# Storing a whole tile at once near the end: two stores fewer and other completion counters for the last two

## The chip, the cores and the metric

The kernel runs on one core of a Trainium2 chip. The metric is the time of one execution on the device in microseconds (us); three runs of the kernel before took 392.55, 392.9 and 393.38 us. Inside the core several engines work side by side, each with its own instruction stream: TensorE (PE, matrix products; PEld is its weight load), VectorE (DVE), ScalarE (ACT), GpSimd (POOL) and SyncE (SP). SP computes nothing here; it issues transfers and waits. ACT can issue transfers too. The transfers themselves are carried out by 16 DMA engines. Engines and transfers are ordered by semaphores, which are counters that one side raises and the other waits for.

## What is computed

The reference is attention followed by a gated two-layer network:

```python
scores = (1.0 / np.sqrt(q.shape[-1])) * np.matmul(q, k.transpose(0, 1, 3, 2))
scores = scores - np.max(scores, axis=-1, keepdims=True)
attn = np.exp(scores)
attn = attn / (np.sum(attn, axis=-1, keepdims=True) + 1e-09)
attn_out = np.matmul(attn, v)                     # 8 batches, 12 heads, 448 tokens, 64
x = attn_out.transpose(0, 2, 1, 3).reshape(8 * 448, 12 * 64)
h = x @ w_in                                      # 3584 x 2048
g = h * (1.0 / (1.0 + np.exp(-h)))
out = g @ w_out                                   # 3584 x 768, float32
```

## The kernel before

A small planner inside the kernel (class `Order`) walks through time with estimated costs, decides which engine does which operation next, and emits the instructions in that order. The order that comes out is fixed when the program is built. The work runs from attention, batch by batch, through the first product (`w_in`) and the gate to the second product (`w_out`), which is the only part that the change and the prediction touch.

The second product is organised in 14 quads, numbered `qd` = 0 to 13 (`LAST` is 13). A quad covers two tiles of 128 token rows (`i` = 0 and 1) and both halves of the 768 output columns (`j` = 0 and 1, 384 columns each), so it yields four output tiles of 128 rows by 384 columns in float32. Instead of eight blocks of products a quad uses seven, in the manner of a fast 2 by 2 matrix product; `product` (its matmuls all carry line 492) accumulates each into a PSUM bank. An output tile then comes into SBUF as an `ost` tile in up to two steps: `take_copy` (ACT, line 768) copies a bank, `take_sum` (DVE, line 774) adds a second bank in place. Three of the four tiles are finished by a sum; the tile (1, 0), the last one of a quad, is finished by the copy of product 4. The step that finishes a tile calls `store` at once.

`store` (lines 745 to 763) cuts the 128 rows into 4 pieces of 32 rows, because the tokens of batches 0 to 6 are held in another order than in `out`: a group of 32 rows goes to every 14th row. In batch 7, the last one, the tokens are in natural order, so neighbouring pieces can go out together, 64 rows at a time. Tiles are counted within pairs of batches (896 rows, 7 tiles), so that the tiles of the last pair are: tiles 0 to 2 in batch 6, tile 3 half in batch 6 and half in batch 7, and tiles 4 to 6 wholly in batch 7. Tile 3 and tile 4 belong to quad 12, tiles 5 and 6 to quad 13. The stores of quads 12 and 13 alternate between SP and ACT as issuing engine (the expression for `eng` in line 760); all earlier ones are issued by SP.

Each of these stores carries one of eight completion counters, here called counter 0 to 7; the framework gives them out in turn, in program order. A store raises its counter by 16 in all when its data has landed, and before it is issued, the issuing engine waits until the previous store on the same counter has landed. After the last instruction of the kernel the framework adds an end sequence (all of it has line 1554): SP waits, in a fixed order and two counters at a time, for every semaphore of the program, first for two counters of GpSimd's transfers, then for counters 0, 1, 2 and so on to 7 of the stores, each paired with another semaphore. Then it waits once more for GpSimd, and then all engines meet at a barrier, the semaphores are cleared, and they meet again. In the kernel before, the last two stores of the program (the two halves of the last tile) carry counter 0 (the one from ACT) and counter 1 (the one from SP).

Of the kernel before, what the change touches and what calls it, by code (L numbers as in the profile page):

```python
# [169 lines left out]
def kernel(  # L170
# [44 lines left out]
    LAST = NT * B // 4 - 1  # L215
# [514 lines left out]
    def take_plain(t, j):  # L730
        nc.scalar.copy(out=ost(t // 2, t % 2, j), in_=pr_t[("o", t, j)][:, 0:OH])
        store(t // 2, t % 2, j)
# [14 lines left out]
    def store(qd, i, j):  # L747
        u, t = divmod(2 * qd + i, NT)
        w, turn = 0, 0
        while w < 4:  # L750
            r, col = divmod(128 * t + 32 * w, S)
            b = 2 * u + r
            dst = out[b * S : (b + 1) * S, OH * j : OH * (j + 1)]
            if b == B - 1:
                n = 2
                dst = dst[col : col + 32 * n]
            else:
                n = 1
                dst = dst.rearrange("(i g) m -> g i m", g=TPP)[col // 32]
            eng = nc.scalar if turn % 2 and 4 * qd + 8 >= NT * B else nc.sync  # L760
            eng.dma_start(out=dst, in_=ost_t[(qd, i, j)][32 * w : 32 * (w + n), :])
            w, turn = w + n, turn + 1
# [4 lines left out]
    def take_copy(qd, m):  # L767
        nc.scalar.copy(out=ost(qd, *OUT[m]), in_=bank(qd, BANK[m]))  # L768
        if m == 4:
            store(qd, *OUT[m])  # L770

    def take_sum(qd, m):
        t = ost_t[(qd, *SUM[m])]
        nc.vector.tensor_tensor(out=t, in0=bank(qd, BANK[m]), in1=t, op=ALU.add)  # L774
        store(qd, *SUM[m])
# [697 lines left out]
    while True:  # L1473
# [44 lines left out]
        if warm["on"] and od.free["PE"] <= od.now and wait > 0.06 and od.now > 0.9:  # L1518
            each = mm(128) if od.now > COLD else 0.107
            n = max(1, int((wait - 0.06) / each), int(wait / each + 0.9) * (od.now < COLD))  # L1520
            if warm.pop("first", None):
                n = FIRST
# [36 lines left out]
```

## Time and profile before

| | |
|---|---|
| three runs | 392.55, 392.9, 393.38 us; median 392.9 |
| time of the profiled execution | 392.49 us |
| span of the profiled execution, first to last instruction | 390.7 us |
| TensorE busy (matmul) | 384.3 us, 98% of the span |
| VectorE, ScalarE, GpSimd busy | 274.6, 253.7, 89.1 us |
| stores of `out` by SP | 194 of 48 KB, 8 of 96 KB |
| stores of `out` by ACT | 2 of 48 KB, 6 of 96 KB |

The span leaves out 1.79 us of the profiled execution's own time (392.49 - 390.7), which lie before its first and after its last recorded instruction. The views give times from the start of the span. A row of the timeline shows start, duration, engine, line, operation, destination and source, count, and in brackets how long the engine had been idle and what ended it; an engine's name with a `q` stands for its sequencer, the part that issues transfers and waits for semaphores. The duration of a transfer's row there is that of its issue, not of its data. "To landing" is the time from the start of the issue until the counter has its full value.

### The profile page before, as it was taken

The page shows a single profiled execution, that of the slowest core. Times are in us where ns is not written, and L with a number is a line of the kernel's source. Part 1 is how long each engine was busy: PE and PEld are TensorE (multiplying, and loading weights), DVE is VectorE, ACT ScalarE, POOL GpSimd, SP SyncE. Part 2 cuts the span into 40 slices and gives each one's busy share as a digit, 9 for nine tenths or more (in the row PEclk, how much of TensorE's full clock was granted, in tenths as well). Part 3 has the DMA queues.
Part 4 walks back from the last instruction along what each step waited for, and adds up shares of the span by engine and source line. Part 5 has one row for each costly group of instructions (what it writes and reads, how often), then busy time and mean ns, then how long its engine had stood idle before and what let it go on. Part 6 is the DMA issues. An engine that isn't in the chain of part 4 may idle for free.

```text
span 390.7 us, 10672 instructions
## 1 busy us (share of the span) xinstructions
PE 384.3 (98%) x4369; PEld 206.3 (53%) x4369; DVE 274.6 (70%) x570; ACT 253.7 (65%) x399; POOL 89.1 (23%) x173
## 2 busy tenths in 40 slices
PE   8999999999999999999999999999999999999995
PEld 7667774444454444545445444544445655556663
DVE  2466676999996877987588758666869984447441
ACT  4988885697766779666774676466783238882220
POOL 7632365415006243400643014000000000000000
PEclk9999999999999999999999999999999999999999
DMA  7999999929039582814956139002100131001333
GB/s 114 202 210 210 159 161 190 187 42 139 1 62 151 121 105 40 119 47 89 145 82 88 40 73 168 7 0 59 27 0 3 42 93 29 0 3 41 92 95 98
DMA packets 35361, 34.52 MB, mean 88 GB/s; under 512 B 11376, under 2 KB 33776, under 8 KB 35312
## 3 DMA queue, kind: packets, MB, share of 16 engines
q0 software_dynamic: 24784, 22.82, 39.5%
q1 hardware_dynamic: 9952, 10.33, 9.8%
q8 instruction: 34, 0.56, 0.6%
q10 hardware_dynamic: 576, 0.69, 0.6%
q14 instruction: 15, 0.12, 0.1%
HBM read 45.61 MB, written 11.01 MB: 145 GB/s over the span
## 4 chain that ended last, share of the span: by engine, by line
PE 97%; DMA 1%; ACT 1%; issue 0%; POOL 0%; DVE 0%; POOLq 0%
PE p L492 31%; PE h L492 29%; PE s L346 13%; PE a L409 11%; PE f L492 8%; PE o L492 3%; PE a L425 2%; DMA rq<-in_q_dram 1%; PE z L1468 1%; ACT E L383 1%; POOL rk L255 0%; ACT ost L768 0%; DVE rq L333 0%; ACT th L518 0%; POOLq L1543 0%
## 5 line engine op out<-in xcount | busy, mean ns | idle before, releaser
L383 ACT ACTIVATE E<-s 128x896 f16<-128x896 f32 (+1 forms) x172 | 149.8, 915 | 38.0 <-PE s L346 36.5
L492 PE MATMUL h<-xT,w_in_t 128*32 128x448 f16 (+2 forms) x1086 | 117.2, 336 | 0.0
L492 PEld LDWEIGHTS <-w_in_t 128*128 128x128 f16 (+1 forms) x1158 | 71.2, 97 | 56.3 <-issue 11.5
L518 ACT ACTIVATE th<-h 128x448 f16<-128x448 f32 (+1 forms) x112 | 54.2, 493 | 36.8 <-PE h L492 31.1
L553 DVE SCALAR_TENSOR_TENSOR G<-th,h 128x448 f16<-128x448 f16 (+2 forms) x112 | 55.7, 509 | 23.4 <-ACT th L518 21.7
L492 PEld LDWEIGHTS <-G 128*128 128x128 f16 (+1 forms) x580 | 43.1, 98 | 32.4 <-issue 4.6
L768 ACT COPY ost<-p 128x384 f32<-128x384 f32 x52 | 24.9, 480 | 53.5 <-PE p L492 47.1
L346 PE MATMUL s<-rq,KT 32*128 32x448 f16 (+4 forms) x768 | 51.0, 337 | 0.8 <-ACT E L383 0.4
L280 POOL DMA_DIRECT2D V<-in_v_dram x88 | 48.3, 559 | 14.2 <-DMA w_out_t<-in_moe_w_out_dram 6.8
L492 PE MATMUL p<-w_out_t,G 128*128 128x384 f16 (+1 forms) x352 | 49.5, 326 | 0.0
L409 PE MATMUL a<-E,V 128*32 128x448 f16 (+2 forms) x864 | 42.3, 333 | 0.0
L492 PEld LDWEIGHTS <-S 128*128 128x128 f16 (+1 forms) x408 | 30.0, 98 | 22.7 <-issue 2.3
L261 POOL DMA_DIRECT2D rq<-in_q_dram x27 | 15.1, 558 | 102.6 <-PE s L346 79.0
L492 PE MATMUL p<-D,S 128*128 128x384 f16 (+1 forms) x256 | 37.2, 326 | 0.0
L774 DVE TENSOR_TENSOR ost<-p,ost 128x384 f32<-128x384 f32 x39 | 21.6, 554 | 18.7 <-PE p L492 14.9
L480 DVE SCALAR_TENSOR_TENSOR xT<-a,rdn 128x448 f16<-128x448 f32 (+1 forms) x54 | 30.4, 569 | 5.8 <-PE a L409 3.6
L346 PEld LDWEIGHTS <-KT 32*128 32x128 f16 (+2 forms) x864 | 17.5, 98 | 29.1 <-issue 27.3
L409 PEld LDWEIGHTS <-V 128*32 128x32 f16 (+1 forms) x864 | 20.5, 96 | 18.8 <-issue 7.6
L394 DVE TENSOR_TENSOR T<-E,E 128x1792 f16<-128x1792 f16 x20 | 21.7, 1084 | 8.0 <-ACT E L383 8.0
L394 DVE TENSOR_TENSOR T<-T,E 128x1792 f16<-128x1792 f16 x20 | 21.7, 1083 | 5.7 <-ACT E L383 5.7
L315 DVE STREAM_TRANSPOSE KT<-rk 128x256 f32<-128x256 f32 (+3 forms) x48 | 16.6, 385 | 6.7 <-DMA rk<-in_k_dram 5.9
L492 PE MATMUL p<-w_out_t,S 128*128 128x384 f16 (+1 forms) x152 | 19.1, 326 | 0.0
(67 smaller groups left out, 321.1 us busy)
## 6 DMA issues: line engine op xcount, KB each, us to landing
out_dram<-ost SPq DMA_DIRECT2D x194, 48.0 KB, 1.6
rk<-in_k_dram POOLq DMA_DIRECT2D x24, 224.0 KB, 5.8
rq<-in_q_dram POOLq DMA_DIRECT2D x21, 224.0 KB, 5.7
w_in_t<-in_moe_w_in_dram POOLq DMA_DIRECT2D x6, 512.0 KB, 11.2
w_out_t<-in_moe_w_out_dram POOLq DMA_DIRECT2D x4, 768.0 KB, 13.5
V<-in_v_dram POOLq DMA_DIRECT2D x43, 64.0 KB, 3.7
V<-in_v_dram POOLq DMA_DIRECT2D x40, 48.0 KB, 4.0
out_dram<-ost SPq DMA_DIRECT2D x8, 96.0 KB, 2.1
```

The costliest lines, as they stand in the source:

```text
L280: nc.gpsimd.dma_start(out=VT[b][32 * x : 32 * (x + 1), hs, 0:count, :], in_=v[b, hs].rearrange("h (i g) d -> i h g d", g=TPP)[:, :, first ...
L315: nc.vector.transpose(out=pairs[:, x:y, 0:count], in_=t[:, first : first + count * (y - x)].rearrange("p (x c) i -> p x c i", c=count),)
L346: nc.tensor.matmul(out=pS[p0 : p0 + 32 * (x1 - x0), h % 2, at : at + nq], lhsT=KT[(b, hg)][32 * h : 32 * (h + 1), c, x0:x1, :, e], rhs=QT[ ...
L383: nc.scalar.activation(out=E[(n, w)][0:kr, 2 * y : 2 * y + 2, 0:nk], in_=pS_t[(n, w, y)][0:kr, :, 0:nk], func=AF.Exp, scale=attn_scale,)
L394: nc.vector.tensor_tensor(out=T[n], in0=T[n] if step else E[(n, 0)], in1=E[(n, step + 1)], op=ALU.add,)
L409: nc.tensor.matmul(out=a[32 * h : 32 * (h + 1), 0:nq], lhsT=w, rhs=e[k0:k1, h, at : at + nq], start=start, stop=stop,)
L480: nc.vector.scalar_tensor_tensor(out=x3(b, cc)[:, cc % 3, 32 * g0 : 32 * g1], in0=acc[(n, part)][:, 0:nq], scalar=0.5, in1=rdn_t[n].rearra ...
L492: nc.tensor.matmul(out=out[i : i + cut], lhsT=w[:, i : i + cut], rhs=x, start=start, stop=stop, skip_group_check=True,)
L518: nc.scalar.activation(out=th, in_=h_t[(b, f, t0)][:, 0 : t1 - t0], func=AF.Tanh)
L553: nc.vector.scalar_tensor_tensor(out=dst[:, f, at + lo : at + hi], in0=th_t[(b, f, t0)][:, lo - t0 : hi - t0], scalar=1.0, in1=h_t[(b, f, ...
L768: nc.scalar.copy(out=ost(qd, *OUT[m]), in_=bank(qd, BANK[m]))
L774: nc.vector.tensor_tensor(out=t, in0=bank(qd, BANK[m]), in1=t, op=ALU.add)
```

## The change

The change lets `store` send out all 128 rows at once when a tile begins in the last batch, except in the last quad:

```diff
             if b == B - 1:
-                n = 2
+                n = 4 if w == 0 and qd < LAST else 2
                 dst = dst[col : col + 32 * n]
```

It applies where the first piece (`w` = 0) of a tile lies in batch 7 and the quad isn't the last one. That is tile 4 of the last pair, the second tile of quad 12, with its two outputs (1, 1) and (1, 0). Each of them was stored as 64 rows from SP and 64 rows from ACT; each is now stored as 128 rows from SP. The first tile of quad 12 keeps its three stores (32, 32 and 64 rows), and the tiles of quad 13 keep their two of 64 rows each. The program then has 208 stores instead of 210. Since the counters are given out in turn, the stores that follow move along by up to two places: the last two stores of the program now carry counter 6 (ACT) and counter 7 (SP). The order of the computing instructions on every engine is the same; ACT issues two transfers fewer. The end sequence has the same waits in the same order.

## Prediction

> **What bounds the kernel now.** I read the page first (share of each engine, and the chain of work that ended last), then that chain over the last 26 us, then the timeline there.
>
> ```profile
> span 390.7 us, 10672 instructions
> PE 384.3 (98%) x4369; PEld 206.3 (53%) x4369; DVE 274.6 (70%) x570; ACT 253.7 (65%) x399; POOL 89.1 (23%) x173
> ...
> PE 97%; DMA 1%; ACT 1%; issue 0%; POOL 0%; DVE 0%; POOLq 0%
> ```
>
> TensorE is busy for 98% of the span, and 97% of the chain is its work. A change of stores can matter only where TensorE waits for one, or after TensorE's last instruction. The chain from 365 us on settles the first:
>
> ```profile
> 3 pieces in order of time: start us, us, what
> 364.98 21.46 PE p L492 x132
> 386.44 0.02 issue
> 386.46 0.48 ACT ost L768
> ```
>
> From quad 12 to the end TensorE runs 132 matmuls in 21.46 us without a break (0.163 us each), so no store holds it up. The chain's last piece is the copy that finishes the last tile; it ends at 386.94, and 3.8 us of the span remain. They hold the last two stores and the end sequence (timeline from 385 us):
>
> ```profile
> 385.81 0.50 ACTq L761 DMA_DIRECT2D out_dram<-ost  x1
> 386.46 0.48 ACT L768 COPY ost<-p 128x384 f32<-128x384 f32 x1 [4.72 <-PE p L492]
> 386.97 0.50 ACTq L761 DMA_DIRECT2D out_dram<-ost  x1
> ...
> 386.97 0.47 SPq L761 DMA_DIRECT2D out_dram<-ost  x1
> ```
>
> How long these last two stores, and the two before them, took to land is in the view of line 761, cut to 386.9-387.1 us and to 385.8-385.9 us, in that order:
>
> ```profile
> DMA to landing us min/median/max: 2.1/2.3/2.4
> ...
> DMA to landing us min/median/max: 2.2/2.3/2.4
> ```
>
> The later one of the last pair lands at 386.97 + 2.4 = 389.37, the pair before it by 385.81 + 2.4 = 388.21. The view of line 1554 (the end sequence) on SP's queue, cut into stretches, shows what follows. The rows are of 387.4-387.52, 389.36-389.41, 389.41-389.84, 389.41-389.79 and 389.84-389.95 us; from 387.51 to 389.36 it has none.
>
> ```profile
> L1554 SPq EVENT_SEMAPHORE  x1: 28/28/28, 387.5 to 387.5; - x1
> ...
> L1554 SPq EVENT_SEMAPHORE  x1: 28/28/28, 389.4 to 389.4; - x1
> ...
> L1554 SPq EVENT_SEMAPHORE  x7: 28/28/28, 389.4 to 389.8; - x7
> ...
> L1554 SPq EVENT_SEMAPHORE  x6: 28/28/28, 389.4 to 389.7; - x6
> ...
> L1554 SPq DRAIN  x2: 7/7/7, 389.9 to 389.9; - x2
> ```
>
> One wait passes at 387.5 (the pair of GpSimd's counters). The next one, on counter 0, passes only at 389.4, and seven more follow it, for counters 1 to 7, whose stores other than the last on counter 1 had landed by 388.21. SP's waits say what it stood for:
>
> ```profile
> SPq L1554 <- DMA out_dram<-ost: 1.8, 1, 1.8
> ```
>
> So the end is a chain in series: last copy, last store's landing (2.4), eight waits one after another, barrier. The eight waits come after the landing because the store that lands last is the one that is asked for first.
>
> **The change, part by part.**
>
> The counters. With the last two stores on counters 6 and 7, SP can pass its waits for 0 to 5 while the last pair is still under way: the latest store among those six is the pair issued at 385.81, landed by 388.21, which leaves 389.37 - 388.21 = 1.16 us for waits of 0.06 us. Only the waits for 6 and 7 stay behind the landing at 389.37: two instead of eight, six fewer. The price of a wait: the wait on counter 0 starts within 389.36-389.41 and that on counter 7 within 389.79-389.84 (it is in the stretch to 389.84 and not in the one to 389.79). Seven steps are therefore 0.38 to 0.48 us, one 0.054 to 0.069; I take the middle, 0.061. Six steps are 0.33 to 0.41, taken as 0.37 us. All of it lies on the path, provided nobody else reaches the barrier later than SP. The latest of the others is ACT, whose row of line 1554 in 387-389 us is
>
> ```profile
> L1554 ACTq DRAIN  x1: 625/625/625, 387.5 to 387.5; - x1
> ```
>
> It ends by 388.2, 1.3 us before SP would get there (about 389.5), so SP remains the last and the gain is whole.
>
> A page bears on this price. The Trainium skill, Advanced Engine Details and Errata, section Miscellaneous Facts, puts reading a semaphore from a sequencer at 50 to 100 ns; by that page the six waits would be worth an estimated 0.30 to 0.60 us. The trace's 54 to 69 ns lies at the low end of it and decides.
>
> The two stores of 128 rows. No store of that size is in the trace. These rows are of quad 12's sum and copy and of the quad after it: rows of several cuts of the timeline, then the view of line 761 over the whole span.
>
> ```profile
> 375.61 0.53 SPq L761 DMA_DIRECT2D out_dram<-ost  x1
> 376.06 0.48 ACT L768 COPY ost<-p 128x384 f32<-128x384 f32 x1 [3.42 <-PE p L492]
> 378.62 0.84 SPq L761 DMA_DIRECT2D out_dram<-ost  x2
> 378.62 0.38 ACTq L761 DMA_DIRECT2D out_dram<-ost  x1
> 379.18 0.48 ACT L768 COPY ost<-p 128x384 f32<-128x384 f32 x1 [2.64 <-PE p L492]
> 379.68 0.47 SPq L761 DMA_DIRECT2D out_dram<-ost  x1
> 379.69 0.50 ACTq L761 DMA_DIRECT2D out_dram<-ost  x1
> 380.23 0.48 ACT L768 COPY ost<-p 128x384 f32<-128x384 f32 x1 [0.57 <-PE p L492]
> 383.22 0.47 SPq L761 DMA_DIRECT2D out_dram<-ost  x1
> ...
> L761 SPq DMA_DIRECT2D out_dram<-ost x202: 314/419/1737, 65.1 to 387.0; - x101
> ...
> DMA to landing us min/median/max: 1.5/1.6/6.1
> ```
>
> The issue: 64 rows take SP 0.47 us, so 128 rows at least that; at most 1.74, the longest issue in the trace. I take twice a 64-row issue, 0.94, since that is the row nearest in kind. The landing: at least 2.4 us, what two 64-row stores issued together (the same bytes) took; at most 6.1, the longest of all. I take 3.0, between 2.4 and twice 2.3, nearer to the pair that moves the same bytes. The Trainium skill, DMA: Bandwidth & Descriptors, section on the anatomy of one DMA, fits a time of 2.0 us and the bytes over 436 GB/s for GpSimd's transfers, which would be an estimated 2.45 us; no run here shows it for a store of this size.
>
> Who is queued behind them: on SP, the wide store of output (1, 1) starts at about 375.6 and the next store at 378.62; the wide store of (1, 0) starts at 379.68 and the next at 383.22. Even 1.74 us of issue leaves 1.3 and 1.8 us. Nobody overwrites the two tiles: quad 13 uses other buffers. By counter: in the built program the wide store of (1, 0) takes counter 7, and the last store of SP must wait for it. With 3.0 us it has landed at 382.7, with 6.1 at 385.8, and it is asked for at 386.97. Cost: nothing, with 1.2 us of cover in the worst row; if it were later than that, each microsecond would be one at the end.
>
> The two issues that ACT loses (0.50 us each). The one at 379.69 stood before a copy, which can start up to 0.5 us earlier. That frees a PSUM bank earlier, but TensorE waited for none, so it is worth nothing. The other fell into the idle time ahead of ACT's copy at 376.06. What is late next is as before: each copy waits for its product.
>
> A wait that is added. ACT no longer learns through its own stores that old stores on counters 5 and 6 have landed, so one wait on these two (both landed long ago, in quad 11) stands ahead of the last copy. ACT is free at 385.81 + 0.50 = 386.31; the copy starts at 386.46, released by TensorE. That is 0.15 us of room for one wait. The nearest row is SP's step of 0.054 to 0.069; two such steps ahead of the copy at 379.18 fitted between the end of ACT's issue (378.62 + 0.38 = 379.00) and that copy, at most 0.18 in all. So it costs 0, and at most 0.18 - 0.15 = 0.03 us; a gain is excluded, since the copy is already released by TensorE. I take 0.
>
> The sum: -0.37 + 0 + 0 + 0 = -0.37 us (bounds -0.41 to -0.30). Against the profiled execution's own 392.49 that is 392.12. This execution was 0.41 us below the median of the runs, 392.9; on the median it is 392.53, and I forecast **392.5 us**, -0.1%.
>
> **The rivals.**
>
> No change at all (392.9). The waits could hide behind something else that ends late: another engine at the barrier, or a wait for counter 6 or 7 that is itself slow. For it: nothing on the page. Against it: ACT's row above ends 1.3 us early, and the drain of SP follows its eighth wait at once, at 389.9.
>
> A larger gain. The end sequence after the landing is 390.7 - 389.37 = 1.33 us in all, of which eight waits are at most 0.55 (8 x 0.069); even all of them would bring -0.55, 392.35. A gain over 0.2% (0.79 us, about what a measurement of this kernel can tell from no change) can't come from the waits as the trace prices them. By the upper end that the Trainium skill gives in Miscellaneous Facts (Advanced Engine Details and Errata) the six would be an estimated 0.60, 392.3; the trace speaks against it. What can carry the result beyond the bound is the scatter of the measurement: single runs lie 0.83 us apart (392.55 to 393.38).
>
> Slower: the wide store of output (1, 0) holds up the last store of SP through counter 7. It decides from a landing 386.97 - 379.68 = 7.29 us after its issue, and outweighs the gain from 7.29 + 0.37 = 7.66 us. With four times the pair's 2.4 us, 9.6, the last store would start 2.3 us late and the kernel take 392.9 + 2.3 - 0.37 = 394.8. For it: the size has no row, and one queue now does what two did. Against it: the longest of all SP's stores landed in 6.1 us, and from 379.7 to 383.2 no other store is issued.
>
> **How the numbers follow.** The waits fall away and nothing else changes: 0.84. No change: 0.07. A dearer wait or a further gain at the end: 0.06. The wide store holds up the end: 0.03. The chances of the verdict need the scatter too. The median of three runs out of a spread of 0.83 us is uncertain by some 0.3, the difference of two medians by some 0.4. With a true -0.37, the difference falls below -0.79 about one time in four (a fifth by the scatter alone, somewhat more since three runs tell little of it), within the bound seven times in ten, and above it rarely. From the first case 0.22 faster, 0.58 same, 0.04 slower; from no change 0.01, 0.05, 0.01; from the larger gain 0.05 and 0.01; from the rival 0.03 slower. That is 0.28, 0.64 and 0.08. The range reaches 0.7 below and 0.6 above the forecast, 391.8 to 393.1: it holds the bounds of the sum, no change and the scatter, and leaves out the slower rival and the far ends of the scatter.
>
> **What the profile after would show.** TensorE's 132 matmuls still without a break up to about 386.4. On SP's queue in line 1554, one wait at 387.5 and six by about 388.3 (the sixth once the pair issued at 385.81 has landed), then two at about 389.4 and 389.5, the drain at 389.5 instead of 389.9, and a span of 390.3. Among the transfers, SP issues two stores of 192 KB and six of 96 KB (202 in all, as before), and ACT six instead of eight. Wrong would be: the last copy later than 386.5 against TensorE's end (the added wait costs), a last store of SP later than 386.97 (counter 7 holds it), or eight waits still behind the last landing (the counters are not what I read).

## The result, and the profile after

| | kernel before | changed kernel |
|---|---|---|
| median of 22 runs each | 392.79 us (392.06 to 393.38) | 392.02 us (391.66 to 392.67) |
| ratio | | 0.9985, 95% interval 0.9978 to 0.9991 |
| profiled execution, own time | 392.49 us | 392.65 us |
| its span | 390.7 us | 390.8 us |

By this ratio the changed kernel is faster by 0.15% (0.09 to 0.22%), which is 0.59 us of 392.79 with an interval of 0.35 to 0.86; the two medians as they stand lie 0.77 us apart. The profiled execution of the changed kernel is among its slowest runs, and its span is not shorter than that of before. Where that comes from is seen in the first copy of an output tile (timeline of each kernel around 65 us, first the kernel before, then the changed one):

```profile
64.64 0.47 ACT L731 COPY ost<-o 128x384 f32<-128x384 f32 x1
```

```profile
65.18 0.47 ACT L731 COPY ost<-o 128x384 f32<-128x384 f32 x1
```

The changed kernel is 0.54 us late here, some 310 us before the first store that the change touches, and 0.51 us late at the last copy (386.97 against 386.46). So the delay arose in the first 65 us, where the two kernels have the same instructions. The last copy starts anywhere from 386.06 to 386.97 us in the nine profiled executions of this document, so a shift of this size is scatter between executions; all times below are therefore counted from the last copy. The end of the chain, and the timeline from there:

```profile
365.00 21.95 PE p L492 x135
386.95 0.02 issue
386.97 0.48 ACT ost L768
...
386.97 0.48 ACT L768 COPY ost<-p 128x384 f32<-128x384 f32 x1 [4.72 <-PE p L492]
387.48 0.50 ACTq L761 DMA_DIRECT2D out_dram<-ost  x1
...
387.48 0.47 SPq L761 DMA_DIRECT2D out_dram<-ost  x1
```

TensorE still runs without a break (135 matmuls in 21.95 us, 0.163 each), the last copy follows its end at once, and the last pair is issued 0.51 us after the copy's start, as before. The landing of that pair (line 761 at 387.4-387.6 us), and then SP's waits in line 1554 in the stretches 387.9-388.4, 388.4-389.5, 389.5-390.0 and 390.0-390.08 us:

```profile
DMA to landing us min/median/max: 2.1/2.3/2.4
...
L1554 SPq EVENT_SEMAPHORE  x5: 28/28/28, 388.0 to 388.3; - x5
...
L1554 SPq EVENT_SEMAPHORE  x2: 28/28/28, 388.7 to 388.8; - x2
...
L1554 SPq EVENT_SEMAPHORE  x2: 28/28/28, 389.9 to 389.9; - x2
...
L1554 SPq DRAIN  x2: 7/7/7, 390.0 to 390.1; - x2
```

The last store lands at 387.48 + 2.4 = 389.88. Five waits passed by 388.3 (GpSimd's pair and counters 0 to 3), two more at 388.7 when the pair issued at 386.3 had landed (counters 4 and 5), and only two stand behind the last landing, where the kernel before had eight. From the start of the last copy to the end of the span it is 390.8 - 386.97 = 3.83 us; before it was 390.7 - 386.46 = 4.24. The page rounds spans to 0.1 us, so such a stretch is good to 0.05. Unrounded, the traces' spans are 390.84 and 390.71 us, which makes 3.87 and 4.25: 0.37 us less, the size of six waits.

### The profile page after: what moved, and what is told of

It is laid out like the page before. It is cut to its first block, busy times and chain, and to the rows that moved or that the text cites. A ratio compares the mean times of both kernels' runs of the same rounds, so it can differ in the third digit from the quotient of the medians.

```text
span 390.8 us, 10670 instructions
## 1 busy us (share of the span) xinstructions
PE 384.9 (98%) x4369; PEld 206.8 (53%) x4369; DVE 274.6 (70%) x570; ACT 253.8 (65%) x399; POOL 89.1 (23%) x173
## 4 chain that ended last, share of the span: by engine, by line
PE 98%; ACT 1%; issue 0%; DVE 0%
PE p L492 31%; PE h L492 29%; PE s L346 13%; PE a L409 11%; PE f L492 8%; PE o L492 3%; PE z L1468 2%; PE a L425 2%; ACT E L383 1%; ACT ost L768 0%; ACT th L518 0%; DVE zeros L228 0%
```

## The experiments

The theory: the time behind the last landing is the number of waits that the end sequence still has to do, 0.061 us each, and nothing else of the change counts. The rival: the wider stores and ACT's lost issues are what pays. Stores of quad 5, some 160 us before the end, serve to move the counters: each store of 32 rows that is cut into two of 16 moves all later stores by one counter.

```diff
+    CUTS = {(5, 1, 0): 4, (5, 0, 1): 2}
...
-            eng.dma_start(out=dst, in_=ost_t[(qd, i, j)][32 * w : 32 * (w + n), :])
+            if w < CUTS.get((qd, i, j), 0):
+                for lo in (0, 16):
+                    eng.dma_start(
+                        out=dst[lo : lo + 16],
+                        in_=ost_t[(qd, i, j)][32 * w + lo : 32 * w + lo + 16, :],
+                    )
+            else:
+                eng.dma_start(out=dst, in_=ost_t[(qd, i, j)][32 * w : 32 * (w + n), :])
```

With these lines the stores stand at line 770, the copies at 777 and the end sequence at 1563. Four kernels were timed beside the kernel before (392.48 us in these runs).

**The counters alone.** The kernel before with the `CUTS` above, six more stores.

> All of the kernel before is kept, the pairs of 64-row stores too (no store of 128 rows); six stores of 32 rows in quad 5 are cut into two of 16, so that the last two stores take counters 6 and 7. Theory of the waits (what is saved is six waits behind the last landing): two waits of line 1554 behind the last landing, as in the changed kernel, the stretch from the start of the last copy to the end of the span 3.87 us instead of 4.25, time 0.37 us below the kernel before. Rival (the gain is that of the wider stores and of the issues that ACT loses): that stretch stays at 4.25 us, no gain.

Measured: 392.07 us, ratio 0.9986 (0.9977 to 0.9995). The last copy in the chain, the span, and the waits of line 1563 in 389.0-389.3 us:

```profile
386.24 0.48 ACT ost L777
...
span 390.1 us, 10684 instructions
...
L1563 SPq EVENT_SEMAPHORE  x2: 28/28/28, 389.1 to 389.2; - x2
```

Two waits behind the landing and 390.1 - 386.24 = 3.86 us from the copy to the end. The whole gain is there without a single store of 128 rows, and with eight stores more than the changed kernel has. The timing alone allows 0.2 to 0.9 us; the trace narrows it to the six waits.

**The merging alone.** The changed kernel with `CUTS = {(5, 1, 0): 2}`, 210 stores as before.

> The changed kernel with its two stores of 128 rows and ACT's two issues fewer, but two stores of 32 rows in quad 5 are cut in two, so that the last two stores take counters 0 and 1 again. Theory of the waits: eight waits behind the last landing, 4.25 us from the start of the last copy to the end, the same time as before (0.0). Rival (the wider stores pay): 3.87 us and 0.4 to 0.6 us faster than before.

Measured: 392.50 us, ratio 0.9998 (0.9989 to 1.0007). The same views, the waits in 389.3-389.9 us:

```profile
386.43 0.48 ACT ost L777
...
span 390.7 us, 10674 instructions
...
L1563 SPq EVENT_SEMAPHORE  x8: 27/28/28, 389.3 to 389.8; - x8
```

Eight waits, 390.7 - 386.43 = 4.27 us, no gain. The rival falls: the trace shows no gain from the wider stores and ACT's two issues fewer by themselves. The timing agrees, though its interval alone would still allow 0.4 us.

**Half of the way.** The kernel before with `CUTS = {(5, 1, 0): 3}`, the last two stores on counters 3 and 4.

> The kernel before with three stores of 32 rows in quad 5 cut in two: the last two stores take counters 3 and 4. Theory of the waits: three waits pass before the last landing and five remain behind it, so half of the gain: 4.25 - 3 x 0.061 = 4.07 us from the start of the last copy to the end, 0.18 us below before, too little for the timing and enough for the trace. Rival: 4.25 us, or a step that is not in proportion to the waits.

Measured: 392.22 us, ratio 0.9993 (0.9984 to 1.0001), which the timing alone can't tell from no change. The waits in 389.0-389.6 us:

```profile
386.29 0.48 ACT ost L777
...
span 390.3 us, 10679 instructions
...
L1563 SPq EVENT_SEMAPHORE  x5: 28/28/28, 389.2 to 389.4; - x5
```

Five waits and 390.3 - 386.29 = 4.01 us, against 4.07 expected; with the unrounded span, 390.33, it is 4.04. Eight, five and two waits give 4.25, 4.04 and 3.87 us from unrounded spans (two waits also 3.86 in the kernel with the counters alone).

**Wide stores at the end too.** In the changed kernel the two stores of 128 rows had turned out quicker than a pair (line 761 at 376.1 and at 380.2 us):

```profile
L761 SPq DMA_DIRECT2D out_dram<-ost x1: 521/521/521, 376.1 to 376.1; - x1
DMA to landing us min/median/max: 2.1/2.1/2.1
...
L761 SPq DMA_DIRECT2D out_dram<-ost x1: 398/398/398, 380.2 to 380.2; - x1
DMA to landing us min/median/max: 1.9/1.9/1.9
```

At the place where a landing counts, the last tile, the change had kept pairs. This kernel stores quad 13 wide as well, with `CUTS = {(5, 1, 0): 4}` to bring the last store to counter 7:

```diff
-                n = 4 if w == 0 and qd < LAST else 2
+                n = 4 if w == 0 else 2
```

> The changed kernel with the tiles of the last quad stored 128 rows at a time too, by SP alone, and four stores of 32 rows in quad 5 cut in two, so that the very last store takes counter 7. In the changed kernel a store of 128 rows landed 1.9 to 2.1 us after its issue, and the later one of the last pair of 64 rows 2.4 us. If that holds for the last store too, the landing comes 0.3 to 0.45 us earlier and one wait instead of two stands behind it (0.06): 3.4 to 3.5 us from the start of the last copy to the end, 0.7 to 0.85 us below the kernel before. If a wide store is quick only where nothing else is on the way, the same, since nothing else is on the way at the end. If the landing is set by the bytes alone: 2.4 us, and 0.43 below the kernel before.

Measured: 391.58 us, ratio 0.9974 (0.9963 to 0.9985) to the kernel before. The last copy, the span, the last store (line 770 at 386.7 us), and line 1563 in 387.0-387.6 and 387.6-388.6 us:

```profile
386.22 0.48 ACT ost L777
...
span 389.5 us, 10670 instructions
...
L770 SPq DMA_DIRECT2D out_dram<-ost x1: 333/333/333, 386.7 to 386.7; - x1
DMA to landing us min/median/max: 1.9/1.9/1.9
...
L1563 SPq EVENT_SEMAPHORE  x8: 28/28/28, 387.1 to 387.5; - x8
...
L1563 SPq EVENT_SEMAPHORE  x1: 28/28/28, 388.6 to 388.6; - x1
```

The store is issued in 0.33 us and lands in 1.9 instead of 2.4; eight waits pass meanwhile and one stands behind it. From the copy to the end: 389.5 - 386.22 = 3.28 us, 0.96 less than before, somewhat more than the 0.7 to 0.85 expected, because the landing came 0.5 us earlier and not 0.3 to 0.45. The bytes are the same as the pair's, so they alone don't set the landing. This version is faster than the kernel before. Its trace puts it ahead of the changed kernel too, 3.28 instead of 3.83 us; the two weren't timed side by side, and the intervals of their ratios overlap.

**Why the wide store is quick.** Three kernels with one execution each: 392.56, 391.92 and 391.37 us in the order below, beside 392.76 for the kernel before. Single times settle little here, so the traces are compared. The first issues both halves of a tile in quad 13 from SP (the rest as in the changed kernel):

```diff
-            eng = nc.scalar if turn % 2 and 4 * qd + 8 >= NT * B else nc.sync
+            eng = nc.scalar if turn % 2 and 4 * qd + 8 >= NT * B and qd < LAST else nc.sync
```

> The changed kernel, but in the last quad both stores of 64 rows of a tile are issued by SP, one after the other, instead of one by SP and one by ACT. It asks why one store of 128 rows (1.86 us to landing in e4_all_wide) beats two of 64 rows issued together (2.1 and 2.4). Theory A, two issuing engines at the same moment hold each other up: the first of the two stores lands after 1.6 to 1.85 us, between 32 rows (1.5) and 128 rows (1.86). Theory B, a store of 64 rows is slow in itself, since its rows lie in half of the partitions: the first lands after 2.1 us as before, and the second, issued 0.4 us later, about 2.5 us after the first issue or later, so that the end comes 0.1 us later than in the changed kernel or more.

Measured: from the last copy to the end 390.7 - 386.47 = 4.23 us, 0.4 more than the changed kernel. The first halves of the last two tiles (line 770 at 385.8 and 387.0 us) and the second half of the last tile (at 387.6):

```profile
L770 SPq DMA_DIRECT2D out_dram<-ost x1: 467/467/467, 385.8 to 385.8; - x1
DMA to landing us min/median/max: 2.1/2.1/2.1
...
L770 SPq DMA_DIRECT2D out_dram<-ost x1: 550/550/550, 387.0 to 387.0; - x1
DMA to landing us min/median/max: 2.2/2.2/2.2
...
L770 SPq DMA_DIRECT2D out_dram<-ost x1: 593/593/593, 387.6 to 387.6; - x1
DMA to landing us min/median/max: 2.2/2.2/2.2
```

Theory A falls: with ACT issuing nothing, a store of 64 rows still takes 0.47 to 0.59 us to issue and 2.1 to 2.2 to land, longer than one of 128 rows, so issuing engines that hold each other up are not the cause. Theory B, that a store of 64 rows is slow in itself, fits, with one rest: the two halves of a tile still overlap in this kernel, and no run here has a half tile alone. The nearest rows speak against the overlap as the cause. In the kernel before, SP issues stores of 32 rows about every 0.46 us (line 761 in 366.5-370 us), so that each has two or three others under way beside it, and they land in 1.5 to 1.6 us:

```profile
L761 SPq DMA_DIRECT2D out_dram<-ost x8: 315/419/421, 366.5 to 369.9; - x8
...
DMA to landing us min/median/max: 1.5/1.6/1.6
```

What in a half tile makes it slow was not taken apart further. That its rows lie in half of the partitions is not enough as a reason, since these stores of 32 rows lie in a quarter of them and land sooner.

The second kernel is the one with wide stores at the end, but quad 13 is issued by ACT:

```diff
-            eng = nc.scalar if turn % 2 and 4 * qd + 8 >= NT * B else nc.sync
+            eng = nc.scalar if (turn % 2 and 4 * qd + 8 >= NT * B) or qd == LAST else nc.sync
```

> As e4_all_wide (stores of 128 rows in the last quad, four stores in quad 5 cut in two, the last store on counter 7), but the last quad's stores are issued by ACT instead of SP. If ACT's stores are as quick as SP's, 1.86 us to landing and 3.28 us from the start of the last copy to the end, as in e4_all_wide; if a store from ACT takes longer in itself (2.4 against 2.1 us in the pairs), about 0.2 to 0.3 us more.

```profile
386.85 0.48 ACT L777 COPY ost<-p 128x384 f32<-128x384 f32 x1 [4.72 <-PE p L492]
...
L770 ACTq DMA_DIRECT2D out_dram<-ost x1: 338/338/338, 387.4 to 387.4; - x1
DMA to landing us min/median/max: 1.9/1.9/1.9
```

Its span is 390.1 us, so 390.1 - 386.85 = 3.25 us, and the landing is 1.9: ACT's store is as quick as SP's.

The third leaves the cuts out, so that it is the changed kernel with the one condition `qd < LAST` removed, and its last store takes counter 3.

> As e4_all_wide but without the stores cut in two: the last store takes counter 3. Theory of the waits: five waits behind the last landing instead of one, 3.28 + 4 x 0.061 = 3.53 us from the start of the last copy to the end; the landing stays at 1.86 us. If cutting the stores of quad 5 had a part in the quick landing, it is longer.

```profile
386.06 0.48 ACT ost L768
...
span 389.6 us, 10662 instructions
...
L1554 SPq EVENT_SEMAPHORE  x5: 27/28/28, 388.4 to 388.7; - x5
```

Five waits behind the landing (line 1554 in 388.35-388.9 us) and 389.6 - 386.06 = 3.54 us, as expected (3.53). So the quick landing goes with the store's width and not with the cuts, and the counter is worth what it was worth before.

## Why the prediction was right

**The counters: right.** Six waits fewer behind the last landing, 0.061 us each. Two, five and eight waits gave 3.87, 4.04 and 4.25 us, and the merging without the counters gave nothing. The Trainium skill's 50 to 100 ns for reading a semaphore (Advanced Engine Details and Errata, Miscellaneous Facts) agrees at its low end with the 0.061 us per wait in these traces.

**The size on the clock: inside the range, in its lower part.** I forecast -0.37 us and 392.5; the measured difference is -0.59 with an interval of 0.35 to 0.86, the median 392.02. The forecast lies just inside the interval, and the gain lies within the 0.2% that I had named as about what a measurement can tell from no change. The traces give 0.37. The kernel with the counters alone has nearly the same ratio, 0.9986, so whatever lies beyond 0.37 needs no merging. It isn't outside the span: the time that the span leaves out is 1.73 to 1.85 us in the 22 runs of the changed kernel and in the 29 of the kernel before that were timed beside the experiments. No row shows a further saving inside the span, and the interval is wide enough for scatter alone; more isn't shown. My absolute number also leaned on the median of three runs, 392.9, while 22 runs have 392.79. That 392.02 fell inside 391.8 to 393.1 owes something to the room that the range left for scatter; what bears out the mechanism is the stretch behind the last copy.

**That no other engine is late at the barrier, and that the end yields no more than the waits: right.** SP's drain follows its last wait at once, at 390.0, and the stretch behind the last copy is shorter by the six waits alone.

**The cover of the wide store: right; its size: wrong.** I took 0.94 us of issue, with 0.47 as the lower bound, and 3.0 us of landing, with 2.4 as the lower bound. Measured were 0.52 and 0.40 us of issue and 2.1 and 1.9 of landing, below the bound in three of four. The step that failed is the assumption that 128 rows take at least as long as the nearest rows of 64: to issue at least as long as one store of 64, to land at least as long as a pair. In these runs 64 rows are the slow width. It cost the sum nothing, since nobody waited for these stores, but it hid the larger gain, the same width on the last tile. The Trainium skill, DMA: Bandwidth & Descriptors, section Rules for kernel authors, says that two transfers to disjoint partition halves share the same engines and serialize, and advises one transfer over 128 partitions. The runs agree with the advice (1.9 us for one store, 2.4 for the pair). That the halves serialize is not what they show: the half that lands first takes 2.1 us, already longer than a whole tile. The Trainium skill's fit for GpSimd's transfers (DMA: Bandwidth & Descriptors, anatomy of one DMA) had given an estimate of 2.45 us, too high for these stores from SP, which landed after 1.9 to 2.1.

**The wait added ahead of the last copy: right.** It stands there (line 768 in 386.8-387.2 us) and the copy is still released by TensorE:

```profile
L768 ACTq EVENT_SEMAPHORE  x1: 38/38/38, 386.9 to 386.9; - x1
...
  PE p L492: 4.7, 1
```

**ACT's issue that fell away: right.** The copy that was at 380.23 is at 380.47 in a run that is 0.51 us late, so 0.27 us earlier, and TensorE shows no trace of it.

**The span of 390.3 that I named as a mark: wrong**, because it took the start of the execution for fixed; the start alone moved by 0.54 us.

## What to carry to other kernels

When a kernel ends on a store, what follows its landing is in series with everything: look at which semaphore the end sequence asks for first, and let the store that lands last be the one that is asked for last. Make the last transfer the one with the shortest landing, which need not be the one with the fewest rows, and read that from transfers of the same width. A gain smaller than the scatter between executions is best shown by counting from the last computing instruction to the end, with a dose of the suspected cause (two, five, eight waits), rather than by the total.

## What was not expected of the hardware

A store of half a tile (64 rows of 1536 bytes from 64 partitions) took longer than one of a whole tile: 0.47 to 0.59 us to issue and 2.1 to 2.2 to land with ACT issuing nothing, against 0.33 us and 1.9 us for 128 rows, while 32 rows landed in 1.5 to 1.6. Split between SP and ACT the halves had both landed after 2.4 us. Issued one after the other by SP they took 387.62 + 2.2 - 387.02 = 2.8 us. Those of 64 and 128 rows are stores of the last quad; the two wide stores of quad 12 took 0.40 and 0.52 us to issue.
